# All engine orders, buffer places and engine choices of a fused attention and channel-mix kernel written anew

## The chip, the cores and the metric

The kernel runs on one core of one Trainium2 chip. The metric is the device time of one execution in microseconds (us). Three runs of the kernel before took 166.07, 166.12 and 166.47 us; the median is 166.12 us. Matrix products run on TensorE (PE; PEld is its weight load), elementwise work on VectorE (DVE), ScalarE (ACT) and GpSimd (POOL), and SyncE (SP) issues nearly all transfers. SBUF is the on-chip memory that all of them read; PSUM holds the results of PE.

## The reference

The reference is windowed attention with four sink positions, and behind it a channel mix with a token shift. The inputs q, k and v are 4 batches x 8 heads x 768 positions x 64, in float32.

```python
keep = (pos[None, :] < 4) | ((rel >= 0) & (rel < 128))      # rel = query - key
scores = where(keep, scale * q @ k.T, -1e9)                 # scale = 1/8
x = softmax(scores) @ v                                     # heads side by side: (4, 768, 512)
x_prev = x shifted by one position, zeros at the start
xk = mu_k * x + (1 - mu_k) * x_prev
xr = mu_r * x + (1 - mu_r) * x_prev
kk = maximum(xk @ w_k, 0) ** 2                              # 512 -> 1024
out = sigmoid(xr @ w_r) * (kk @ w_v)                        # 1024 -> 512
```

## The kernel before, in words

The work is cut into 12 units of 256 positions (4 batches x 3), numbered 0 to 11. A unit goes through four stages, and the stages of neighbouring units run at the same time.

- **Prepare.** ks, qs and vs are loaded in float32 (256 KB to each transfer, issued by SP). Casts to bfloat16 make kb, qb (lines 536 and 543, two halves each) and vb (line 646, two halves). kb and qb are then turned into kt and qt, either by PE through a PSUM bank (line 576) with a copy out of it (line 589), or by a transposing transfer on SP's queue (line 562): k of units 4 to 11 and q of units 8 to 11 go the second way.
- **Attend.** In four chunks of two heads: scores on PE into sc (line 721), exponential on ACT into e (line 775), a mask on DVE (line 789), values on PE (line 808), reciprocal and scaling on DVE into x (lines 822 and 825). Units 0 and 1 have no mask on DVE; PE adds a bias to sc ahead of the scores (line 728) from a tile that GpSimd builds at the start (line 418, named ob there). Sink keys are copied by GpSimd into ksink once per batch (line 670).
- **Mix.** x is transposed into xt (line 849, or by transfer in units 9 to 11), td is the difference of neighbouring positions (line 877), and xk and xr are each built by four scalar-tensor-tensor instructions (line 888).
- **Channel mix.** Keys on PE (line 939), rl by a relu out of the bank (line 949 on ACT or 953 on DVE), kk by a square (line 967 on ACT or 963 on DVE), the gate on PE (line 979) with a tanh on ACT (line 985), the value product on PE (line 997, and 909 for the last 128 positions), and one DVE instruction that multiplies both (lines 1006 and 919) ahead of the store. The weights wk, wr and wv come in float32 and are cast once, at the start (lines 501, 505 and 507).

While PE would be idle early on, it multiplies a tile of zeros named warm (line 1018), which I call fills below.

Nothing decides the order at run time. Every step is recorded as an operation with a number, and three tables written out by hand or by a planner decide the rest. `CHOICE` gives the engine for the operations that have a choice, `SLOTS` the buffer of each tile in the order of recording, and `ORDER` the sequence in which operations are emitted; a negative number is a fill. Each engine runs its own instructions in that sequence and waits in place when an input or a buffer is not ready. The four `bank` buffers, the two `sc` buffers and the SP queue are the scarcest. In the names of the order rows below, the digit behind a tile's name is its buffer, not its unit.

Of the kernel before, what the change touches and what calls it, by code (L numbers as in the profile page):

```python
# [18 lines left out]
    92: "ACT", 93: "ACT", 94: "ACT", 95: "ACT", 97: "ACT", 100: "ACT", 102: "DVE", 105: "DVE",  # L19
    110: "DVE", 111: "DVE", 114: "ACT", 115: "DVE", 139: "POOL", 142: "POOL", 145: "POOL", 148:  # L20
    "DVE", 150: "DVE", 151: "ACT", 152: "ACT", 154: "DVE", 161: "DVE", 191: "DVE", 193: "DVE",
    194: "DVE", 197: "DVE", 199: "DVE", 200: "DVE", 203: "DVE", 204: "DVE", 213: "DVE", 230:
    "ACT", 234: "ACT", 273: "DVE", 276: "DVE", 279: "DVE", 282: "DVE", 285: "ACT", 286: "ACT",
    298: "DVE", 306: "DVE", 315: "ACT", 354: "DVE", 364: "ACT", 365: "DVE", 367: "DVE", 383:
    "ACT", 387: "ACT", 436: "DVE", 439: "DVE", 444: "DVE", 445: "DVE", 467: "ACT", 475: "ACT",
    514: "DVE", 516: "DVE", 521: "DVE", 524: "ACT", 525: "ACT", 546: "ACT", 550: "ACT", 554:
    "ACT", 558: "ACT", 595: "DVE", 598: "DVE", 603: "ACT", 604: "ACT", 606: "DVE", 634: "ACT",
    681: "DVE", 682: "DVE", 691: "DVE", 700: "ACT", 704: "ACT", 708: "ACT", 755: "DVE", 759:
    "DVE", 760: "ACT", 772: "DVE", 781: "ACT", 785: "ACT", 789: "ACT", 834: "DVE", 836: "DVE",
    837: "DVE", 853: "ACT", 856: "DVE", 857: "ACT", 860: "DVE", 861: "ACT", 904: "DVE", 906:  # L30
    "DVE", 910: "DVE", 912: "DVE", 913: "DVE", 929: "ACT", 933: "ACT", 940: "DVE", 941: "ACT",
    994: "DVE", 995: "ACT", 999: "ACT", 1003: "ACT", 1007: "ACT", 1022: "DVE", 1026: "DVE",
# [113 lines left out]
)  # L146


# [926 lines left out]
```

## Time and profile before

| what | value |
|---|---|
| median of three runs | 166.12 us |
| span of the profiled execution, first to last instruction | 164.3 us |
| median less span | 1.8 us |
| PE busy | 158.4 us in 1603 matrix products, 30 of them fills |
| DVE busy | 145.4 us |
| ACT busy | 131.2 us |
| POOL busy | 13.5 us, 9.9 of them in the first 24 us |
| mean granted TensorE clock | 0.999 |

The profile gives the span of the profiled execution and no other time of it; the 1.8 us are taken as lying outside the first and the last instruction. A line of groups reads: line, engine, operation, output<-input, sizes, count, then busy time in us and mean ns of one, then the idle time of the engine ahead of them and what ended it. A row of the timeline reads: start, duration, engine, line, operation, count. A row of windows has, for every engine, busy us and the number of instructions in that stretch. PE's matrix products overlap in the pipeline and their ends are modelled, so PE's busy share hides short waits.

### The profile page before, as it was taken

The page shows a single profiled execution, that of the slowest core. Times are in us where ns is not written, and L with a number is a line of the kernel's source. Part 1 is how long each engine was busy: PE and PEld are TensorE (multiplying, and loading weights), DVE is VectorE, ACT ScalarE, POOL GpSimd, SP SyncE. Part 2 cuts the span into 40 slices and gives each one's busy share as a digit, 9 for nine tenths or more (in the row PEclk, how much of TensorE's full clock was granted, in tenths as well). Part 3 has the DMA queues.
Part 4 walks back from the last instruction along what each step waited for, and adds up shares of the span by engine and source line. Part 5 has one row for each costly group of instructions (what it writes and reads, how often), then busy time and mean ns, then how long its engine had stood idle before and what let it go on. Part 6 is the DMA issues. An engine that isn't in the chain of part 4 may idle for free.

```text
span 164.3 us, 4195 instructions
## 1 busy us (share of the span) xinstructions
PE 158.4 (96%) x1603; PEld 102.6 (62%) x1603; DVE 145.4 (89%) x381; ACT 131.2 (80%) x218; POOL 13.5 (8%) x38
## 2 busy tenths in 40 slices
PE   6999889999999999999999999999999999999992
PEld 2455568866467587577566775856575765664851
DVE  5259999999999999989999999999999999789752
ACT  3277999999999999999999999997668759163240
POOL 6409300010000000060000000000000000000000
PEclk9999999999999999999999999999999999999999
DMA  4999999999969896999999887986996955077743
GB/s 120 247 305 311 348 335 355 301 354 210 228 154 270 135 240 148 234 198 167 224 216 157 188 156 163 235 146 150 199 123 136 362 149 200 0 90 297 262 185 128
DMA packets 79042, 34.60 MB, mean 211 GB/s; under 512 B 67112, under 2 KB 73520, under 8 KB 79024
## 3 DMA queue, kind: packets, MB, share of 16 engines
q1 hardware_dynamic: 79008, 34.35, 86.3%
q8 instruction: 12, 0.20, 0.6%
q14 instruction: 6, 0.05, 0.1%
q10 hardware_dynamic: 16, 0.00, 0.0%
HBM read 24.12 MB, written 6.29 MB: 185 GB/s over the span
## 4 chain that ended last, share of the span: by engine, by line
PE 79%; ACT 8%; SPq 4%; DMA 3%; issue 2%; DVE 1%; POOL 1%; DVEq 0%; ACTq 0%; POOLq 0%
PE bank L997 23%; PE bank L939 23%; PE bank L979 12%; PE bank L808 6%; PE sc L721 6%; SPq L337 3%; DMA qs<-in_q_dram 3%; PE bank L576 2%; ACT e L775 2%; PE bank L849 2%; ACT rl L949 1%; PE bank L763 1%; ACT qt L589 1%; PE bank L909 1%; PE bank L1018 1%
## 5 line engine op out<-in xcount | busy, mean ns | idle before, releaser
L775 ACT ACTIVATE e<-sc 128x1024 bf16<-128x1024 f32 (+1 forms) x48 | 46.1, 994 | 1.8 <-PE sc L721 1.7
L939 PE MATMUL bank<-xk,wk_sb 128*128 128x256 bf16 x384 | 47.1, 273 | 0.0
L997 PE MATMUL bank<-wv_h,kk 128*128 128x512 bf16 x184 | 43.1, 379 | 0.1
L939 PEld LDWEIGHTS <-wk_sb 128*128 128x128 bf16 x384 | 36.4, 98 | 7.4 <-issue 0.4
L949 ACT ACTIVATE rl<-bank 128x512 bf16<-128x512 f32 x40 | 24.2, 625 | 8.6 <-PE bank L939 7.1
L997 PEld LDWEIGHTS <-kk 128*128 128x128 bf16 x184 | 17.1, 98 | 17.8 <-issue 0.4
L789 DVE TENSOR_TENSOR e<-e,mask 128x1024 bf16<-128x1024 bf16 (+1 forms) x40 | 25.4, 642 | 0.7 <-ACT e L775 0.5
L979 PE MATMUL bank<-wr_sb,xr 128*128 128x512 bf16 x96 | 23.7, 379 | 0.0
L888 DVE SCALAR_TENSOR_TENSOR xk<-td,mu_all,xt 128x256 bf16<-128x256 bf16 x48 | 22.4, 483 | 0.3
L888 DVE SCALAR_TENSOR_TENSOR xr<-td,mu_all,xt 128x256 bf16<-128x256 bf16 x48 | 22.1, 475 | 0.2
L967 ACT ACTIVATE kk<-rl 128x512 bf16<-128x512 bf16 x29 | 18.3, 664 | 4.2 <-DVE rl L953 4.0
L985 ACT ACTIVATE th<-bank 128x512 f32<-128x512 f32 x24 | 15.1, 646 | 5.7 <-PE bank L979 5.7
L825 DVE TENSOR_TENSOR x<-bank,rec 128x256 bf16<-128x256 f32 x48 | 19.2, 416 | 0.4
L808 PE MATMUL bank<-vb,e 128*128 128x65 bf16 x352 | 16.6, 194 | 0.0
L1006 DVE SCALAR_TENSOR_TENSOR w<-th,bank 128x512 f32<-128x512 f32 x19 | 13.0, 682 | 3.6 <-issue 1.8
L808 PEld LDWEIGHTS <-e 128*128 128x128 bf16 x352 | 13.6, 97 | 3.5
L979 PEld LDWEIGHTS <-xr 128*128 128x128 bf16 x96 | 8.8, 98 | 8.6 <-issue 0.2
L721 PE MATMUL sc<-qt,kt 64*128 64x128 bf16 (+1 forms) x256 | 13.9, 238 | 0.0
L721 PEld LDWEIGHTS <-kt 64*128 64x128 bf16 x256 | 8.9, 94 | 5.7 <-issue 3.1
L1018 PE MATMUL bank<-warm 128*128 128x512 bf16 x30 | 10.6, 484 | 1.1 <-DVE warm L1038 1.1
L877 DVE TENSOR_TENSOR td<-xt 128x512 bf16<-128x512 bf16 x24 | 10.3, 428 | 0.7 <-ACT xt L858 0.5
L589 ACT COPY qt<-bank 128x512 bf16<-128x512 bf16 x15 | 9.4, 643 | 1.0 <-PE bank L576 1.0
(74 smaller groups left out, 161.7 us busy)
## 6 DMA issues: line engine op xcount, KB each, us to landing
ks<-in_k_dram SPq DMA_DIRECT2D x24, 256.0 KB, 4.7
qs<-in_q_dram SPq DMA_DIRECT2D x24, 256.0 KB, 4.4
vs<-in_v_dram SPq DMA_DIRECT2D x24, 256.0 KB, 4.4
out_dram<-w SPq DMA_DIRECT2D x19, 256.0 KB, 2.7
w<-in_moe_w_k_dram SPq DMA_DIRECT2D x2, 1024.0 KB, 10.4
w<-in_moe_w_v_dram SPq DMA_DIRECT2D x2, 1024.0 KB, 9.3
w<-in_moe_w_r_dram SPq DMA_DIRECT2D x1, 1024.0 KB, 9.7
out_dram<-ob SPq DMA_DIRECT2D x4, 256.0 KB, 2.6
```

The source lines that it names most:

```text
L721: nc.tensor.matmul(out=sc[:, a, o0:o1], lhsT=lhs[rows], rhs=rhs[rows], start=u not in BIAS, stop=True, skip_group_check=u in BIAS)
L775: nc.scalar.activation(out=buf[ek][:, :, lo:], in_=buf[sck][:, :, lo:], func=AF.Exp, scale=scale)
L789: nc.vector.tensor_tensor(out=at, in0=at, in1=m, op=ALU.mult)
L808: nc.tensor.matmul(out=o[:, g, a, :], lhsT=e[:, a, e0:e0 + 128], rhs=rhs, start=(T == 0 and i == 0), stop=(i == len(blocks) - 1), skip_gro ...
L825: P.op("DVE", dve(256), lambda ok=ok, rk=rk, c=c: nc.vector.tensor_tensor(out=buf["x", u][:, :, 128 * c:128 * c + 128].rearrange("p g (a d ...
L888: nc.vector.scalar_tensor_tensor(out=buf[key][:, c, :], in0=buf[tk][:, i, :], scalar=mu[w][:, c:c + 1], in1=xt[:, c, t0 - 1:t0 + 255], op0 ...
L939: nc.tensor.matmul(out=ps[:, i, :], lhsT=wk_sb[:, c, 128 * f:128 * f + 128], rhs=xk[:, c, :], start=(c == 0), stop=(c == NC - 1), skip_gro ...
L949: nc.scalar.activation(out=buf[rk], in_=buf[psk].rearrange("p (i t) -> p i t", i=2), func=AF.Relu)
L967: nc.scalar.activation(out=buf["kk", u][:, 2 * f2:2 * f2 + 2, :], in_=buf[rk], func=AF.Square)
L979: nc.tensor.matmul(out=buf[psk], lhsT=buf["xr", u][:, c, 128 * g:128 * g + 128], rhs=wr_sb[:, c, :], start=(c == 0), stop=(c == NC - 1))
L985: P.op("ACT", act(512), lambda psk=psk, tk=tk: nc.scalar.activation(out=buf[tk], in_=buf[psk], func=AF.Tanh, scale=0.5), rank + 4 + g, tak ...
L997: nc.tensor.matmul(out=buf[psk], rhs=wv_h[:, f, :], lhsT=buf["kk", u][:, f, 128 * g:128 * g + 128], start=(f == 0), stop=(f == NF - 1))
```

## The change

The code is the same apart from the three tables, which are longer by 13 lines in all: line N of the kernel before is line N+13 after. What the program does is the same set of operations, with the same loads, products and stores. What differs:

```diff
 CHOICE = {
-    92: "ACT", 93: "ACT", 94: "ACT", 95: "ACT", 97: "ACT", 100: "ACT", 102: "DVE", 105: "DVE",
...
+    92: "DVE", 93: "ACT", 94: "ACT", 95: "POOL", 96: "DVE", 97: "DVE", 98: "ACT", 99: "DVE", 100:
...
 ORDER = (
-    80, 81, 78, 82, 87, 83, 84, 77, -1, -2, -3, -4, -1, -2, 90, 0, 1, 79, 102, 108, -2, -3, -4,
...
+    80, 82, 87, 77, 89, 83, 2, 3, 0, 1, 81, 4, -1, -2, -3, -4, -1, -2, -3, -4, -1, -2, 119, 5, 79,
...
 SLOTS = (
-    0, 0, 0, 1, 1, 0, 1, 1, 2, 0, 1, 2, 2, 2, 0, 0, 0, 1, 1, 1, 2, 2, 0, 0, 0, 2, 1, 1, 1, 2, 2,
...
+    0, 0, 0, 1, 1, 1, 0, 1, 2, 1, 0, 2, 2, 2, 0, 0, 0, 1, 1, 1, 2, 2, 0, 0, 0, 2, 1, 1, 1, 2, 2,
...
```

Counted over the whole program, the instructions that change engine are these:

| instruction | ACT | DVE | POOL |
|---|---|---|---|
| casts to kb | 11 to 5 | 11 to 12 | 2 to 7 |
| casts to qb | 9 to 9 | 14 to 11 | 1 to 4 |
| casts to vb | 11 to 7 | 13 to 10 | 0 to 7 |
| copies to kt and qt | 20 to 22 | 4 to 2 | |
| weight casts (128x1024) | 6 to 4 | 4 to 5 | 0 to 1 |
| relu to rl | 40 to 42 | 8 to 6 | |
| square to kk | 29 to 31 | 19 to 17 | |

The change is described as having casts on GpSimd for the first two units alone. The tables say otherwise: the kernel before has three such casts, all for unit 1, and the changed one has 19, of which seven are for units 0 and 1, one is a weight's, and eleven are for units 3 to 11. The fills go from 30 to 20. SP loads q of the first units ahead of k, the second half of w_k ahead of the first, and it issues the first stores among the loads and no longer behind most of them.

The first place is GpSimd's queue from the bias tile (ob) on. Before, with the casts of unit 1 and three pairs of ksink copies behind them:

```order
L418 AFFINE_SELECT ob2_134<-warm_144 128x128 x2
L451 COPY spread_149<-ident_148 4x4x4 x2
L543 CAST qb1_83<-qs1_71 128x2x4x64
L543 CAST kb1_80<-ks1_68 128x2x4x64
L418 AFFINE_SELECT mask_146<-ones_157 128x128 x2
L543 CAST kb1_80<-ks1_68 128x2x4x64
L470 COPY vsink0_153<-hmask_150 128x8
L470 COPY vsink1_154<-hmask_150 128x8
L670 COPY ksink0_151<-kt0_85 64x4x4 x2
```

After, the same stretch, which begins with the mask that is now built ahead of the bias:

```order
L431 AFFINE_SELECT mask_146<-ones_157 128x128 x2
L431 AFFINE_SELECT ob2_134<-warm_144 128x128 x3
L447 MEMSET ob2_134 4x256
L483 COPY vsink0_153<-hmask_150 128x8
L483 COPY vsink1_154<-hmask_150 128x8
L556 CAST qb0_82<-qs0_70 128x2x4x64
L659 CAST vb0_135<-vs0_73 128x8x64
L464 COPY spread_149<-ident_148 4x4x4 x2
L556 CAST kb0_79<-ks0_67 128x2x4x64
L556 CAST qb1_83<-qs1_71 128x2x4x64
```

The mask's two instructions stand ahead of the bias, and halves of q, v and k of unit 0 come in as casts.

The second place is the rest of GpSimd's queue, which lies in the part of the run where all units are in flight. Before it is only copies of sink keys:

```order
L418 AFFINE_SELECT mask0_147<-ones_157 128x128 x3
L434 MEMSET mask0_147 4x256
L670 COPY ksink1_152<-kt3_88 64x4x4 x2
L670 COPY ksink0_151<-kt2_87 64x4x4 x2
L670 COPY ksink1_152<-kt1_86 64x4x4 x2
```

After, casts of k, q and v stand between those copies:

```order
L549 CAST kb1_80<-ks1_68 128x512
L659 CAST vb2_137<-vs2_75 128x8x64
L549 CAST kb0_79<-ks2_69 128x512
L683 COPY ksink0_151<-kt2_87 64x4x4 x2
L549 CAST qb2_84<-qs2_72 128x512
L549 CAST kb0_79<-ks2_69 128x512
L683 COPY ksink1_152<-kt0_85 64x4x4 x2
L659 CAST vb2_137<-vs1_74 128x8x64
L549 CAST kb2_81<-ks1_68 128x512
```

Casts that DVE and ACT did for the later units now wait their turn on GpSimd.

The third place is ACT's queue at the start, from its first cast. Before:

```order
L543 CAST kb0_79<-ks0_67 128x2x4x64
L589 COPY kt0_85<-bank1_64 128x2x256
L589 COPY qt0_89<-bank2_65 128x2x256
L646 CAST vb0_135<-vs0_73 128x8x64
L775 ACTIVATE e0_93<-sc0_61 128x2x384
L775 ACTIVATE e1_94<-sc1_62 128x2x384
```

After:

```order
L602 COPY qt0_89<-bank0_63 128x2x256
L387 DMA ob2_134<-in_moe_mu_r_dram 4x128
L602 COPY kt0_85<-bank2_65 128x2x256
L602 COPY qt0_89<-bank1_64 128x2x256
L788 ACTIVATE e0_93<-sc0_61 128x2x384
L788 ACTIVATE e1_94<-sc1_62 128x2x384
```

Two casts ahead of the first exponential have left ACT, a copy to qt has come ahead of it, and one small load was moved behind a copy.

More of the change, by code (lines that the diff above doesn't have):

```diff
@@ L25 @@
[L25 to L30, printed above, removed]
@@ L31 @@
[L31 to L32 removed]
+    92: "DVE", 93: "ACT", 94: "ACT", 95: "POOL", 96: "DVE", 97: "DVE", 98: "ACT", 99: "DVE", 100:
+    "ACT", 101: "DVE", 102: "DVE", 104: "ACT", 105: "DVE", 107: "ACT", 108: "POOL", 110: "ACT",
+    111: "POOL", 113: "ACT", 114: "POOL", 115: "DVE", 139: "DVE", 141: "ACT", 142: "DVE", 144:
+    "DVE", 145: "POOL", 147: "ACT", 148: "POOL", 150: "ACT", 151: "POOL", 152: "POOL", 154: "DVE",
@@ new lines @@
+    161: "DVE", 191: "DVE", 193: "ACT", 194: "DVE", 196: "DVE", 197: "DVE", 199: "ACT", 200:
+    "ACT", 202: "ACT", 203: "DVE", 204: "DVE", 206: "DVE", 213: "DVE", 221: "ACT", 222: "ACT",
+    225: "ACT", 226: "DVE", 229: "DVE", 230: "ACT", 233: "ACT", 234: "ACT", 273: "DVE", 275:
+    "ACT", 276: "DVE", 278: "ACT", 279: "DVE", 281: "ACT", 282: "POOL", 284: "ACT", 285: "ACT",
+    286: "ACT", 291: "DVE", 298: "ACT", 306: "ACT", 307: "DVE", 310: "ACT", 311: "DVE", 314:
+    "ACT", 315: "ACT", 318: "ACT", 319: "ACT", 354: "DVE", 356: "DVE", 358: "ACT", 359: "ACT",
@@ new lines @@
+    361: "ACT", 363: "ACT", 364: "ACT", 365: "DVE", 367: "ACT", 374: "ACT", 382: "ACT", 383:
+    "DVE", 386: "ACT", 387: "ACT", 390: "ACT", 391: "ACT", 394: "ACT", 395: "ACT", 434: "ACT",
+    436: "ACT", 438: "ACT", 439: "POOL", 441: "ACT", 443: "ACT", 444: "DVE", 445: "DVE", 447:
+    "DVE", 454: "ACT", 462: "ACT", 463: "ACT", 466: "ACT", 467: "DVE", 470: "ACT", 471: "DVE",
+    474: "ACT", 475: "ACT", 514: "DVE", 516: "ACT", 518: "ACT", 519: "DVE", 521: "DVE", 523:
+    "ACT", 524: "POOL", 525: "DVE", 530: "DVE", 537: "ACT", 545: "ACT", 546: "ACT", 549: "ACT",
@@ L33 @@
+    1007: "DVE", 1022: "DVE", 1023: "ACT", 1026: "DVE", 1027: "DVE", 1030: "ACT", 1031: "DVE",
     1034: "DVE", 1035: "ACT",
```

17 lines of the change are left out of this document (12 added, 5 removed), and 155 rows, old and new, of tables (ORDER, SLOTS).

## The prediction

> **What bounds the kernel now.** I read the page's first part, then the busy time by stage, then the chain of waits, then single instructions where GpSimd and DVE meet.
>
> ```profile
> span 164.3 us, 4195 instructions
> PE 158.4 (96%) x1603; PEld 102.6 (62%) x1603; DVE 145.4 (89%) x381; ACT 131.2 (80%) x218; POOL 13.5 (8%) x38
> ```
>
> PE is the fullest engine, but DVE is close. The stages say where:
>
> ```profile
> 13.00:24.00 11.00, 9.73 (x141) 6.21 (x140) 10.67 (x31) 10.21 (x17) 4.87 (x13) 1.00 1.09 338
> 24.00:60.00 36.00, 35.96 (x384) 24.66 (x385) 35.40 (x93) 35.70 (x59) 0.74 (x2) 1.00 0.98 253
> 60.00:100.00 40.00, 39.89 (x443) 27.27 (x440) 38.16 (x103) 39.57 (x71) 2.89 (x4) 1.00 0.97 190
> 100.00:140.00 40.00, 40.00 (x425) 25.67 (x423) 39.01 (x100) 32.02 (x52) 0.00 (x0) 1.00 0.85 183
> 140.00:161.00 21.00, 21.00 (x145) 13.34 (x142) 15.65 (x35) 7.59 (x13) 0.00 (x0) 1.00 0.52 163
> ```
>
> The columns behind the window's length are PE, PEld, DVE, ACT and POOL. From 24 to 140 us DVE is busy 35.40 + 38.16 + 39.01 = 112.57 of 116 us: it idles 3.4 us in all. ACT is as full until 100 us. So three engines run side by side with hardly a gap, each fed by the others. Only from 140 us on is PE alone, with DVE and ACT in reserve. The chain shows the same:
>
> ```profile
> 65.14 0.93 ACT e L775
> ...
> 68.26 0.49 ACT th L985
> ...
> 148.10 3.45 PE bank L997 x16
> ...
> 152.41 3.49 PE bank L939 x32
> ...
> 159.36 1.76 PE bank L909 x16
> 161.15 0.42 DVE w L919
> ```
>
> Around 65 us it runs over ACT, at the end over PE without a pause, and then the last DVE instruction and its store up to 164.3. PE's products are the same before and after, so the time can move in three places: the start, the waits between 24 and 140 us, and the end. The last is the same in both: the two half products of line 909, two short DVE instructions, two stores. I put it at nothing, since from 140 us PE covers all other work; if that cover went, it would show as idle PE there.
>
> **What DVE and ACT are relieved of.** Prices from the groups:
>
> ```profile
> L646 DVE CAST vb<-vs 128x512 bf16<-128x512 f32 x13 | 5.4, 420 | 0.1
> ...
> L953 DVE TENSOR_SCALAR rl<-bank 128x512 bf16<-128x512 f32 x8 | 5.5, 685 | 1.5 <-PE bank L939 1.5
> ...
> L536 ACT CAST kb<-ks 128x512 bf16<-128x512 f32 x10 | 6.6, 655 | 0.0
> ...
> L501 ACT ACTIVATE wk_sb<-w 128x1024 bf16<-128x1024 f32 x4 | 4.2, 1092 | 0.0
> ```
>
> From the table of the change, DVE loses net 7 instructions of the short kind (2 qb and kb, 3 vb, 2 squares) at 0.42 us and 3 of the long kind (2 copies to kt and qt, 2 relus, less one weight cast) at 0.685: 2.9 + 2.1 = 5.0 us. ACT loses net 4 of the 512-column kind (10 casts, less 2 copies, 2 relus, 2 squares) at 0.655 and 2 weight casts at 1.092: 2.6 + 2.2 = 4.8 us. The means include the tail of an instruction in which the next one already runs, so both sums are upper values. By themselves they would let PE run with fewer waits.
>
> **What GpSimd's casts cost.** GpSimd's casts go from 3 to 19. Four of them (q, v and k of unit 0, q of unit 1) fall before about 13 us, where DVE waits for loads anyway. Of the other 15 the kernel before has two. That is 13 more, and the weight's cast is twice as wide, so 14 at the price of one. The price has two sides: how long GpSimd takes, and how long it holds up DVE.
>
> ```profile
> L543 POOL CAST kb<-ks 128x512 bf16<-128x512 f32 x2 | 1.4, 702 | 0.0
> L543 POOL CAST qb<-qs 128x512 bf16<-128x512 f32 x1 | 0.9, 865 | 6.7 <-DMA qs<-in_q_dram 6.7
> ...
> 13.48 0.62 POOL L543 CAST kb<-ks 128x512 bf16<-128x512 f32 x1
> ...
> 15.01 0.79 POOL L543 CAST kb<-ks 128x512 bf16<-128x512 f32 x1
> ...
> 13.75 0.62 DVE L877 TENSOR_TENSOR td<-xt 128x512 bf16<-128x512 bf16 x1
> ...
> 15.34 0.73 DVE L888 SCALAR_TENSOR_TENSOR xk<-td,mu_all,xt 128x256 bf16<-128x256 bf16 x1
> ...
> L877 DVE TENSOR_TENSOR td<-xt 128x512 bf16<-128x512 bf16 x24 | 10.3, 428 | 0.7 <-ACT xt L858 0.5
> ...
> L888 DVE SCALAR_TENSOR_TENSOR xk<-td,mu_all,xt 128x256 bf16<-128x256 bf16 x48 | 22.4, 483 | 0.3
> ```
>
> The td that met the first cast took 0.62 us where the mean is 0.43; the xk that met the second took 0.73 where the mean is 0.48. Both end the same 0.27 us behind the cast (14.37 after 14.10, 16.07 after 15.80), so DVE seems to have stood still until GpSimd was done. These two lost 0.19 and 0.25 us because they began when the cast was well under way. The other direction is in the middle of the run, where GpSimd only copies 64x16 sink keys:
>
> ```profile
> L670 POOL COPY ksink<-kt x8: 188/196/2303, 16.2 to 96.6; 64x16 bf16<-64x16 bf16 x8
> ...
> 70.30 2.54 POOL L670 COPY ksink<-kt 64x16 bf16<-64x16 bf16 x2 [36.96 <-DMA kt<-kb]
> ...
> 70.25 0.42 DVE L646 CAST vb<-vs 128x512 bf16<-128x512 f32 x1
> 70.59 0.42 DVE L543 CAST qb<-qs 128x512 bf16<-128x512 f32 x1
> 70.93 0.41 DVE L963 TENSOR_TENSOR kk<-rl 128x512 bf16<-128x512 bf16 x1
> 71.26 1.28 DVE L789 TENSOR_TENSOR e<-e,mask 128x1024 bf16<-128x1024 bf16 x2
> 73.05 0.18 DVE L822 RECIPROCAL rec<-bank 128x4 f32<-128x4 f32 x1 [0.51 <-ACT qt L589]
> ```
>
> Columns of the first row are the shortest, the median and the longest in ns. One copy took 2.30 us instead of 0.19: it was issued at 70.30 and ended at 72.60, as DVE's row of back-to-back instructions out of SBUF ended (72.54). So a GpSimd cast in the full part of the run can wait some 2 us, and when it does get its turn, DVE waits.
>
> The page "SBUF — State Buffer" of the Trainium skill, section "Who interferes with whom", states that DVE and GpSimd share one pair of ports as an exclusive lock, that whoever comes first keeps it for its whole instruction, and that DVE takes it for casts and for two inputs out of SBUF but not for one input out of PSUM. By that rule, the trace agrees: the held instructions above are of the first kinds.
>
> Bounds for the loss of DVE per cast: 0.22 us (mean of the two rows above) and 0.62 us (the whole of the shortest cast). Could it be below nothing? No: a cast on GpSimd frees DVE's time, but that is counted above already. In the middle of the run DVE issues back to back, so a cast gets its turn only at a boundary between two instructions and then stands in the way from its first moment; the value is nearer the upper end, yet DVE's instructions out of PSUM (x, reciprocals, relus) can pass. I take 0.45: 14 x 0.45 = 6.3 us, with ends of 3.1 and 8.7. Less the 5.0 relieved, DVE gains 1.3 us of work, with ends of -1.9 and +3.7. With 3.4 us of idle time in 116, all of it waits for others, I let the whole of it reach the end: PE waits for xk, masks and x.
>
> What sits behind: a late vb holds a value product on PE; a late kb holds the transposing transfers on SP's queue and each load and store queued behind them. Loads are issued well ahead, so I add nothing there, up to 2 us for each cast that is late by as much as the copy above.
>
> **The start.**
>
> ```profile
> 7.04 0.39 PE L576 MATMUL bank<-ident,kb 128*128 128x128 bf16 x4
> ...
> 9.54 0.50 PE L721 MATMUL sc<-qt,kt 64*128 64x256 bf16 x8
> ...
> 4.86 0.44 DVE L543 CAST kb<-ks 128x512 bf16<-128x512 f32 x1 [1.43 <-DMA ks<-in_k_dram]
> ...
> 7.61 0.43 DVE L543 CAST qb<-qs 128x512 bf16<-128x512 f32 x1 [2.31 <-DMA qs<-in_q_dram]
> ...
> 4.68 0.30 POOL L434 MEMSET ob<- 4x256 bf16 x1
> ...
> L418 POOL TENSOR_SCALAR_AFFINE_SELECT mask<-ones 128x128 bf16<-128x128 bf16 x5 | 2.0, 429 | 0.1
> ```
>
> The first scores at 9.54 need both k and q; the second of them arrives at 7.6, whichever it is, so loading q first changes nothing there. The bias tile, whole at 4.98 before (the memset's end), comes 2 x 0.43 = 0.9 us later, behind the mask, and is now PE's first real work; at 5.9 us it would still be ahead of 7.6. The transposes of q's other half now wait for a GpSimd cast (0.6 to 0.9 us by the rows above) where DVE had one of 0.42. Against that, ACT and DVE have less ahead of them up to 24 us, and ten fills fewer are queued; a fill fills a wait and costs nothing in itself. I put the start at 0, with ends of -0.8 (ACT rid of two casts) and +0.9 (the mask's delay passed on).
>
> **The sum.** 164.3 + 1.3 + 0 = 165.6 us of span. The profiled execution's span lies 1.8 us under the median, so 167.4 us.
>
> **The rivals.**
>
> A, faster: GpSimd's casts slip between DVE's instructions out of PSUM and cost 0.22 each. Then DVE is relieved by 1.9 us and ACT by up to 4.8, and PE's waits shrink. Since PE is full of its own work from 100 us on, I let three quarters of the 1.9 through: 164.7 us. For it speaks that the chain runs over ACT around 65 us; against it, the 2.3 us of one tiny copy. It decides if the loss per cast is under 5.0 / 14 = 0.36 us.
>
> B, no change: DVE's relief and loss cancel (0.36 each), and the orders are as good as each other: 166.1 us.
>
> C, much slower: DVE loses the whole cast each time, 8.7 less 5.0 is 3.7: 169.8 us. The lock of the page "SBUF — State Buffer", taken to the letter, gives this if every cast meets a DVE instruction of the locked kinds. Or a late cast stops SP's queue or PE for 2 us once or twice, with the same end.
>
> **The numbers.** The forecast (167.4) has a chance of 0.44, C 0.16, B 0.12, A 0.28. Slower by over 0.3% (0.5 us, about what a measurement can tell here) is then 0.60, within it 0.12, faster 0.28. The range of 164.8 to 170.0 leaves out half of A (0.14) and a third of C (0.05). The slower cases alone lie between 166.7 and 170.0.
>
> **What would show it.** GpSimd busy some 12 to 20 us longer, with casts in the middle well over 0.7 us; td, xk, masks and casts on DVE with larger means than 428, 483 and 420 ns; DVE busy no lower than 144 us though ten instructions have left it; ACT near 126. The start is right if the first scores come between 9 and 10.4 us, and the end if PE's last product ends about 3.4 us ahead of the span's end. I am wrong if GpSimd's casts stay at 0.6 us and DVE's means stay put: then A. I am also wrong if the new order leaves PE waiting at places that have nothing to do with GpSimd, which no row of this trace can show.

## The result, and the profile after

The changed kernel takes 177.4 us in the median of four runs (176.7 to 178.2) beside 166.2 for the kernel before on the same chip: 1.067 of it, with a 95% interval of 1.062 to 1.071. The forecast was 167.4, in a range of 164.8 to 170.0. The sign was right and the size was not: 1.2 us were forecast, 11.2 came. The execution profiled is one of the slower ones, 178.2 us, with a span of 176.5.

The first part of the page after, and the share of the DMA engines over the span in 40 slices:

```profile
span 176.5 us, 4175 instructions
...
PE 158.6 (90%) x1575; PEld 102.3 (58%) x1593; DVE 144.8 (82%) x371; ACT 128.2 (73%) x212; POOL 23.8 (13%) x54
...
DMA  3999999799997996698899997799454560067243
```

No engine has more work than before: PE 158.6 us (158.4 before), DVE 144.8 (145.4), ACT 128.2 (131.2). GpSimd has 10 us more, all of it beside the others. (PE's figure holds 7.8 us of fills instead of 10.6; its other products are the same ones and take 3.0 us longer by the profile, some of them at a lower clock, see the last section.) So nearly all of the 12.2 us of span is waiting. Where, the busy time by stage tells; first the kernel before, then the one after (columns: window, PE, PEld, DVE, ACT, POOL, granted clock, share of the DMA engines, GB/s; the share adds up the times of all packets over 16 engines, so it can pass 1):

```profile
0.00:24.00 24.00, 21.48 (x217) 11.69 (x218) 16.75 (x54) 16.31 (x26) 9.86 (x32) 1.00 0.94 277
24.00:50.00 26.00, 25.96 (x272) 18.02 (x272) 25.52 (x66) 25.80 (x43) 0.74 (x2) 1.00 0.97 268
50.00:90.00 40.00, 39.89 (x438) 26.97 (x435) 38.30 (x102) 39.69 (x70) 2.50 (x2) 1.00 0.99 197
90.00:130.00 40.00, 40.00 (x427) 26.45 (x427) 39.08 (x103) 34.21 (x58) 0.39 (x2) 1.00 0.92 179
130.00:160.00 30.00, 30.00 (x252) 18.75 (x249) 24.75 (x59) 15.18 (x25) 0.00 (x0) 1.00 0.56 181
```

```profile
0.00:24.00 24.00, 19.92 (x208) 10.97 (x210) 16.32 (x51) 14.32 (x23) 11.45 (x37) 1.00 0.89 268
24.00:50.00 26.00, 25.07 (x244) 16.59 (x244) 24.95 (x61) 24.86 (x42) 3.63 (x4) 1.00 1.03 277
50.00:90.00 40.00, 35.49 (x392) 23.76 (x396) 33.38 (x88) 33.23 (x58) 3.85 (x7) 0.96 0.85 201
90.00:130.00 40.00, 35.08 (x371) 23.43 (x375) 34.97 (x89) 32.93 (x55) 4.83 (x7) 1.00 0.95 168
130.00:160.00 30.00, 29.72 (x286) 19.44 (x288) 26.71 (x71) 19.27 (x32) 0.00 (x0) 1.00 0.41 119
```

PE loses 4.4 us from 50 to 90 us (39.89 less 35.49), 4.9 from 90 to 130, 0.9 from 24 to 50 and 0.3 from 130 to 160: 10.5 us. The 1.6 us that it is less busy in the first 24 us are no loss: its fills there are 7.15 us instead of 10.48, its other products 12.8 instead of 11.0, and a kernel below that is as fast as the one before (a_quart) is busy 20.1 us there too. DVE and ACT idle in the same stretches, so none of the three holds up the others by its work. The last column but one was there before the change too: the DMA engines' share is 0.92 to 0.99 up to 130 us. After the change it is 0.85 from 50 to 90 us, where PE waits 4.5 us, so a high share alone doesn't make an engine wait.

The chain that ended last, by engine, before and after:

```profile
PE 79%; ACT 8%; SPq 4%; DMA 3%; issue 2%; DVE 1%; POOL 1%; DVEq 0%; ACTq 0%; POOLq 0%
...
PE 57%; DMA 14%; SPq 11%; DVE 10%; ACT 4%; issue 3%; ACTq 0%; DVEq 0%
```

A quarter of it is now transfers and SP's queue (DMA and SPq), where it was 7%. Some of the waits of the engines for transfers (us in total, times, longest), before and then after:

```profile
POOL qb L543 <- DMA qs<-in_q_dram: 6.7, 1, 6.7
...
DVE qb L543 <- DMA qs<-in_q_dram: 2.3, 1, 2.3
...
ACT kb L543 <- DMA ks<-in_k_dram: 1.7, 1, 1.7
...
DVE kb L543 <- DMA ks<-in_k_dram: 1.4, 1, 1.4
```

```profile
PE sc L734 <- DMA qt<-qb: 3.3, 2, 2.1
...
ACT qb L556 <- DMA qs<-in_q_dram: 3.2, 1, 3.2
...
DVE kb L556 <- DMA ks<-in_k_dram: 3.0, 2, 2.8
...
DVE vb L659 <- DMA vs<-in_v_dram: 2.5, 2, 1.3
...
PE bank L589 <- ACT qb L556: 2.3, 1, 2.3
...
ACT qb L549 <- DMA qs<-in_q_dram: 1.7, 1, 1.7
```

Before, DVE and ACT wait 5.4 us for loads, all at the start. After, the row of DVE's kb and one of the two waits of vb are at the start as well, but from 15 us on DVE and ACT wait 8.0 us for loads of q, k and v where they waited for none before, and PE itself stands at a score product for a transposed q. One of them, followed back along SP's queue (the timeline of SP, start, duration, instruction; after):

```profile
49.66 0.57 SPq L320 DMA_DIRECT2D vs<-in_v_dram  x1
50.29 1.33 SPq L350 DMA_DIRECT2D qs<-in_q_dram  x2
51.66 0.61 SPq L330 DMA_DIRECT2D ks<-in_k_dram  x1
52.32 2.65 SPq L320 DMA_DIRECT2D vs<-in_v_dram  x1
55.02 1.49 SPq L330 DMA_DIRECT2D ks<-in_k_dram  x1
56.55 0.92 SPq L320 DMA_DIRECT2D vs<-in_v_dram  x1
57.51 0.79 SPq L350 DMA_DIRECT2D qs<-in_q_dram  x1
```

and the chain of waits goes on from there:

```profile
57.51 3.78 DMA qs<-in_q_dram
...
61.37 0.13 ACT qb L556
```

By the order of the program, the row at 50.29 holds the first half of q of unit 5 and the first half of q of unit 6; the row at 57.51 is the second half of q of unit 5. Between them stand q, k and v of unit 6, k of unit 7 and v of unit 5. ACT waits 3.2 us for that half, until 61.3, and PE waits 2.3 us for ACT's cast before unit 5's transposes (both rows above). Before, both halves of that q were issued one behind the other at 49.0. Half of the loads from 24 us on take 0.66 us or less to issue (0.60 before); here three of them took 2.65, 1.49 and 0.92.

For all 48 half loads of units 4 to 11, the time from their issue on SP's queue to the first cast that reads them, worked out from both traces:

| | least | median | most | under 4.9 us |
|---|---|---|---|---|
| before | 5.0 | 8.1 | 15.4 | 0 |
| after | 3.4 | 7.7 | 31.4 | 7 |

The mean lead is no shorter (8.7 before, 9.4 after). It is uneven: v of unit 9 is issued 31 us ahead of its cast and k of unit 11 29 us, while seven others have at least 0.5 us less than the least that any had before. Three of the seven are read by GpSimd, four by DVE or ACT.

### The profile page after: what moved, and what is told of

The parts are those of the page before. It is cut to its first block, busy times and chain, and to the rows that moved or that the text cites. A ratio compares the mean times of both kernels' runs of the same rounds, so it can differ in the third digit from the quotient of the medians.

```text
span 176.5 us, 4175 instructions
## 1 busy us (share of the span) xinstructions
PE 158.6 (90%) x1575; PEld 102.3 (58%) x1593; DVE 144.8 (82%) x371; ACT 128.2 (73%) x212; POOL 23.8 (13%) x54
## 4 chain that ended last, share of the span: by engine, by line
PE 57%; DMA 14%; SPq 11%; DVE 10%; ACT 4%; issue 3%; ACTq 0%; DVEq 0%
PE bank L952 19%; PE bank L1010 15%; PE bank L992 8%; DMA qs<-in_q_dram 5%; SPq L350 4%; PE sc L734 4%; PE bank L821 4%; SPq L320 4%; DMA qt<-qb 3%; DMA vs<-in_v_dram 3%; DMA ks<-in_k_dram 3%; DVE x L838 2%; PE bank L862 2%; SPq L330 2%; DVE td L890 1%
## 5 line engine op out<-in xcount | busy, mean ns | idle before, releaser
L952 PE MATMUL bank<-xk,wk_sb 128*128 128x256 bf16 x384 | 49.1, 278 | 2.0 <-ACT th L998 2.0
L788 ACT ACTIVATE e<-sc 128x1024 bf16<-128x1024 f32 (+1 forms) x48 | 44.3, 955 | 2.4 <-PE sc L734 2.4
L952 PEld LDWEIGHTS <-wk_sb 128*128 128x128 bf16 x384 | 37.0, 99 | 9.6 <-issue 2.2
L802 DVE TENSOR_TENSOR e<-e,mask 128x1024 bf16<-128x1024 bf16 (+1 forms) x40 | 26.4, 669 | 3.1 <-ACT e L788 3.1
L901 DVE SCALAR_TENSOR_TENSOR xr<-td,mu_all,xt 128x256 bf16<-128x256 bf16 x48 | 23.1, 485 | 0.0
L998 ACT ACTIVATE th<-bank 128x512 f32<-128x512 f32 x24 | 14.4, 606 | 9.1 <-PE bank L992 8.7
L980 ACT ACTIVATE kk<-rl 128x512 bf16<-128x512 bf16 x31 | 19.3, 637 | 1.9 <-DVE rl L966 1.8
L1019 DVE SCALAR_TENSOR_TENSOR w<-th,bank 128x512 f32<-128x512 f32 x19 | 12.8, 681 | 4.0 <-PE bank L1010 2.9
L835 DVE RECIPROCAL rec<-bank 128x4 f32<-128x4 f32 x48 | 7.5, 172 | 7.4 <-PE bank L821 6.7
L890 DVE TENSOR_TENSOR td<-xt 128x512 bf16<-128x512 bf16 x24 | 11.2, 478 | 1.8 <-DMA xt<-x 1.7
L602 ACT COPY qt<-bank 128x512 bf16<-128x512 bf16 x14 | 8.4, 599 | 4.2 <-PE bank L589 4.1
(76 smaller groups left out, 158.6 us busy)
```

Of the source, the lines that this page charges most:

```text
L788: nc.scalar.activation(out=buf[ek][:, :, lo:], in_=buf[sck][:, :, lo:], func=AF.Exp, scale=scale)
L802: nc.vector.tensor_tensor(out=at, in0=at, in1=m, op=ALU.mult)
L901: nc.vector.scalar_tensor_tensor(out=buf[key][:, c, :], in0=buf[tk][:, i, :], scalar=mu[w][:, c:c + 1], in1=xt[:, c, t0 - 1:t0 + 255], op0 ...
L952: nc.tensor.matmul(out=ps[:, i, :], lhsT=wk_sb[:, c, 128 * f:128 * f + 128], rhs=xk[:, c, :], start=(c == 0), stop=(c == NC - 1), skip_gro ...
L980: nc.scalar.activation(out=buf["kk", u][:, 2 * f2:2 * f2 + 2, :], in_=buf[rk], func=AF.Square)
L998: P.op("ACT", act(512), lambda psk=psk, tk=tk: nc.scalar.activation(out=buf[tk], in_=buf[psk], func=AF.Tanh, scale=0.5), rank + 4 + g, tak ...
```

## The experiments

The theories: G, GpSimd's casts cost what was lost; E, the orders of PE, DVE and ACT themselves are worse; L, loads and transposing transfers land late; within L, whether their order on SP's queue alone is at fault or what the engines' orders ask of it. The expectations also name Q (a bad order on SP's queue alone), S (the early stores), P (the places in SP's queue and not the bytes) and M (what one transfer gains another loses, or each order of transfers fits one order of casts). Times are medians beside the kernel before on the same chip (166.0 to 166.5). All kernels differ from the changed kernel or the one before only as shown; where SP's queue is altered, the other engines' orders and choices are untouched. In the diffs, q5.1 is the second half load of q of unit 5, kt and qt are transposing transfers, S a store.

### GpSimd's casts

Taken off GpSimd in the changed kernel, and put on GpSimd in the kernel before:

```diff
 # changed kernel -> a_nogps; kernel before -> b_gps is the reverse
-    282, 439, 524, 593, 679, 751, 755, 836, 837, 904, 912: "POOL"
+    282, 439, 755, 836, 837, 904, 912: "DVE",  524, 593, 679, 751: "ACT"
```

> The changed kernel with the eleven casts of units 3 to 11 that stand on GpSimd given to the engine that had them in the kernel before (seven to VectorE, four to ScalarE), at the same places of the order; nothing else is moved. Theory G: the loss of the change comes from these casts, so the time falls by 6 us or more, to 168 to 171.5. Theory Q: the casts are 0.6 to 0.8 us long in the trace, GpSimd is idle before them waiting for the loads, so the same late loads now hold VectorE and ScalarE, which have other work queued behind: 177 to 180, slower than the changed kernel.

> The kernel before with the eleven casts of units 3 to 11 that the changed kernel has on GpSimd given to GpSimd at their places, seven taken from VectorE and four from ScalarE; nothing else is altered. Theory G: the lock or the length of the casts costs 0.45 us each and what waits for them, 168.5 to 172. Without such a cost VectorE has 2.9 us and ScalarE 2.2 us less to do where both are full: 163.5 to 166.1. In between (165.8 to 167) the relief and the cost of the lock are about even, as the prediction had it.

Measured (ratios are to the kernel before, with a 95% interval): a_nogps 180.1 us (178.8 to 181.8), ratio 1.082 [1.076, 1.088], slower than the changed kernel; b_gps 166.35, ratio 1.002 [0.9996, 1.004]. Theory G falls from both sides. b_gps also gives the price of a cast on GpSimd, which the prediction had estimated. Its page, and two groups of DVE:

```profile
span 164.8 us, 4208 instructions
...
PE 158.4 (96%) x1603; PEld 102.3 (62%) x1603; DVE 146.4 (89%) x374; ACT 130.0 (79%) x214; POOL 21.5 (13%) x49
```

```profile
L804 DVE TENSOR_TENSOR e<-e,mask 128x1024 bf16<-128x1024 bf16 (+1 forms) x40 | 26.1, 663 | 0.9 <-ACT e L790 0.8
L903 DVE SCALAR_TENSOR_TENSOR xk<-td,mu_all,xt 128x256 bf16<-128x256 bf16 x48 | 23.2, 501 | 0.3
```

DVE has seven casts fewer, 7 x 0.42 = 2.9 us, and yet is busy 146.4 us instead of 145.4: its other work grew by 3.9 us, the masks from 642 to 663 ns in the mean, xk from 483 to 501. That is 3.9 / 11 = 0.36 us for each cast on GpSimd, and PE's time does not move. The other way round, a_nogps gives DVE these seven casts back and its busy time goes from 144.8 to 145.0 us, so its other work shrinks by 2.7 us, 0.25 for each cast, in a kernel where DVE idles more. And b_gps too has seven leads under 4.9 us, six of them of loads that GpSimd reads, at the time of the kernel before: a short lead costs nothing where the reader can wait.

### The bytes of the loads

Each load of units 3 to 11 cut to a quarter of its rows, in both kernels, and to a half in the changed one (shown: v; q and k alike):

```diff
-                        out=buf[key][:, g, :, :],
-                        in_=v[b, :, s0:s0 + 128, :].rearrange("h p d -> p h d")), rank,
+                        out=buf[key][:, g, 0:H if u < 3 else 2, :],
+                        in_=v[b, 0:H if u < 3 else 2, s0:s0 + 128, :].rearrange(
+                            "h p d -> p h d")), rank,
```

> The changed kernel with each load of q, k and v of units 3 to 11 cut to a quarter of its rows (the other three quarters of the buffer keep what an earlier unit left there, so attention of these units is computed on partly stale data); number and order of the transfers, casts and products are as they were. Theory L (the loads arrive late because SP's queue issues them in an order that leaves the DMA engines, busy 0.8 to 1.1 of the time up to 120 us, too little time for what is wanted next): with a quarter of the bytes nearly every transfer is early, and the time falls to within 3 us of the same cut made in the kernel before, 164 to 169. Theory E (the orders of VectorE, ScalarE and TensorE themselves are worse): at least 6 us above the cut kernel before, 171 to 176. Theory P (the places of the transfers in the in-order queue, with their waits, not the bytes): 171 to 177, with TensorE waiting at the same places.

> The kernel before with the same cut of each load of units 3 to 11 to a quarter of its rows (attention on partly stale data). The profile of before shows no wait of VectorE, ScalarE or TensorE for a load after the start, so all theories say 163 to 166.5; a gain of more than 3 us would mean that the full queue of transfers costs the kernel before something too.

> The changed kernel with each load of units 3 to 11 cut to half of its rows (attention of these units on partly stale data). If the DMA engines are only a little short of what the order asks (they are busy 0.8 to 1.1 of the time to 120 us), half of the bytes is enough and the time is that of the quarter, 166 to 167.5; if they are far short, half of the loss stays, 169 to 173.

Measured: a_quart 166.3 us, ratio 1.001 [0.998, 1.004]; b_quart 166.0, 0.998 [0.996, 1.001]; a_half 167.5, 1.007 [1.004, 1.009]. With a quarter of the bytes the changed kernel takes the time of the kernel before, and the cut gives the kernel before nothing. The engines' orders, their choices, GpSimd's casts and the number and places of the transfers are the same in a_quart as in the changed kernel; so E and G fall as causes by themselves, and the whole loss comes with transfers that land late. The window from 50 to 90 us in a_quart:

```profile
50.00:90.00 40.00, 39.65 (x468) 27.69 (x467) 39.61 (x103) 38.40 (x66) 6.36 (x9) 1.00 0.47 100
```

The DMA engines are busy 0.47 of the time there and PE waits 0.35 us, against 4.51. Half of the bytes leaves 1.2 us of the 11, so the shortage is not a large one. A quarter of the bytes is also a quarter of the packets, and SP issues faster: from 24 us on 52 loads of q, k and v take 53.5 us to issue in the changed kernel (47.7 in the one before), 51 take 28.1 in a_quart. So this cut doesn't part the DMA engines from the queue that feeds them.

The same cut in units 3 to 7 alone (a_q37), and in units 8 to 11 alone (a_q811):

```diff
-                        out=buf[key][:, g, 0:H if u < 3 else 2, :],
+                        out=buf[key][:, g, 0:H if u < 3 or u > 7 else 2, :],   # a_q37
+                        out=buf[key][:, g, 0:H if u < 8 else 2, :],            # a_q811
```

> The changed kernel with the loads of units 3 to 7 alone cut to a quarter of their rows (attention of these units on partly stale data). Read from the trace of the changed kernel, TensorE waits 8.8 us from 50 to 90 us (1.8 in the kernel before) and 7.2 us from 90 to 130 us (1.3 in the kernel before). If each wait belongs to the loads of its own stretch, the cut takes away the first 7 us: 170 to 172. If the first half's backlog is also what makes the second half late, 166.5 to 169.

> The changed kernel with the loads of units 8 to 11 alone cut to a quarter of their rows. If each wait belongs to the loads of its own stretch, it takes away the second 6 us and a little of the first (some loads of units 8, 9 and 11 are issued between 66 and 92 us): 169 to 171.5. If the waits of the first half come back later as waits that were hidden behind the second, 172 to 175.

Measured: a_q37 169.55 us, ratio 1.018 [1.013, 1.022]; a_q811 168.3, 1.010 [1.006, 1.014]. Gains of 7.9 and 9.1, more together than the 11.1 of both at once, so the two halves share a part. In each, the stretch whose loads were left whole keeps waits; a_q37 first:

```profile
50.00:90.00 40.00, 39.33 (x461) 27.52 (x465) 39.31 (x103) 38.45 (x66) 5.20 (x9) 1.00 0.78 150
90.00:130.00 40.00, 37.35 (x399) 23.89 (x404) 36.79 (x97) 31.75 (x54) 3.56 (x4) 1.00 0.84 167
```

```profile
50.00:90.00 40.00, 37.37 (x438) 25.69 (x442) 37.18 (x98) 36.30 (x63) 4.92 (x9) 1.00 0.82 177
90.00:130.00 40.00, 39.40 (x430) 25.89 (x434) 39.34 (x105) 34.57 (x57) 2.83 (x4) 1.00 0.43 104
```

PE still waits 2.7 us behind 90 us in the first and 2.6 us ahead of it in the second, over half of what the changed kernel waits there (4.9 and 4.5): the rest of each wait went with loads of the other half, which stood in the way.

### Stores among the loads

```diff
  SP, changed kernel -> a_stores:
- q7.1 S0.0 kt6.1 k7.1 S1.1 q8.0 ... q10.1 S4.0 kt10.1 ... v11.0 S3.0 ... kt11.0 S6.0 kt11.1
+ q7.1 kt6.1 k7.1 q8.0 ... q10.1 kt10.1 ... v11.0 ... kt11.0 kt11.1 S0.0 S1.1 S4.0 S3.0 S6.0
  SP, kernel before -> b_stores: S0.0, S1.1, S4.0, S3.0 put behind q7.1, k7.1, q11.1, kt11.0
```

> The changed kernel with the five stores that stand among the loads on SP's queue (issued at 68.6, 72.8, 113.2, 117.4 and 128.4 us) moved behind the last transposing transfer of k; nothing else is moved. Theory S: each store takes 0.6 us of issue and waits up to 2.3 us for its product; two of them stand ahead of late transfers of unit 6, 7, and two ahead of those of unit 10, so 2 to 4 us come back: 173.5 to 175.5. Theory Q: a part of its own sum, 0.5 to 2 us back: 175.4 to 177. Theory G: no change, 176.7 to 178.

> The kernel before with four stores (ob of units 0, 1, 4 and 3) put among the loads at the places that the changed kernel has for them on SP's queue; nothing else is moved. Each store moves 256 KB, some 1.3 us at the 190 GB/s of the stretch from 60 to 120 us. Theory L with leads: the loads of before are issued at least 5.0 us ahead of their cast, 8.2 in the median, so two stores in a row are mostly swallowed: 166 to 168. If the place of a store in the queue, with its wait for its product, holds what is behind it: 168 to 172.

Measured: a_stores 174.45 us, ratio 1.051 [1.044, 1.058], 3 us of the 11 back; b_stores 166.0, ratio 0.999 [0.997, 1.002]. Five such stores cost 3 us in the changed kernel's queue; four cost nothing in the queue of before, whose loads of units 4 to 11 have at least 5.0 us of lead.

### Single transfers put forward

```diff
  SP, changed kernel -> a_five (a_five_st: and the stores as in a_stores):
- q5.0 q6.0 k6.0 v6.0 k7.0 v5.0 q5.1        ... q6.1 k9.0 ... v9.0 v6.1
+ q5.0 q5.1 q6.0 k6.0 v6.0 k7.0 v5.0        ... q6.1 v6.1 k9.0 ... v9.0
- qt8.0 v8.0 v8.1 k10.1 kt8.1 qt8.1         ... q10.0 ... q11.1 q10.1
+ qt8.0 qt8.1 v8.0 v8.1 k10.1 kt8.1         ... q10.0 q10.1 ... q11.1
- qt10.0 v11.0 S3.0 qt10.1
+ qt10.0 qt10.1 v11.0 S3.0
  SP, changed kernel -> a_halves: each second half directly behind its first, 27 moved
```

> The changed kernel (177.4 us) with one thing altered: on SP's queue the load of the second half of each unit's q, k or v (27 of them) stands directly behind the load of its first half; the orders of TensorE, VectorE, ScalarE and GpSimd, the engine choices and the buffers are as they were. Theory Q (SP's queue is in a bad order: a half that is needed soon is issued behind loads that are needed later and behind transposing transfers and stores): the TensorE waits at 58.1 (2.5), 62.3 (1.6), 83.5 (1.4) and 115.9 (1.5 us) hang on second halves of q of unit 5, v of unit 7 and q of unit 10, 7.0 us together, so 170 to 173 us, and the stretch from 60 to 120 loses most of its TensorE waits. Theory G (the casts on GpSimd are what costs, by the lock or by their length): no change, 176.7 to 178. Theory S (the early stores on SP's queue): no change either, 176.5 to 178.

> The changed kernel with five transfers moved forward on SP's queue and nothing else: the second half of q of unit 5 behind its first (issued at 57.5 us in the trace, six transfers behind it), the second half of v of unit 6 behind that of q of unit 6 (79.0 us, 27 us behind its first half), the second transposing transfer of q of unit 8 behind the first (99.3 us, 16 us after its cast), the second half of q of unit 10 behind its first (112.2 us), and the second transposing transfer of q of unit 10 behind the first (118.9 us). Theory L in the form that single transfers stand too late behind ones that are wanted later: the TensorE waits at 58.1, 62.3, 83.5, 99.9, 115.9 and 120.5 us (10.5 us) go in good part, 168 to 173. If the DMA engines are so full that what is put forward makes another transfer late by as much (theory M): 175 to 181.

> The same five transfers put forward, and the five early stores moved behind the last transposing transfer of k. Theory L: what the stores gave (3 us) beside the five, 167 to 170.5. Theory M: 172 to 178.

Measured: a_halves 180.4 us (178.1 to 181.0), ratio 1.082 [1.073, 1.091]; a_five 173.1, 1.039 [1.033, 1.045]; a_five_st 173.8, 1.047 [1.042, 1.052]. The five transfers bring 4.3 us, the stores nothing beside them. Putting all second halves forward, for which theory Q expected 170 to 173, makes it worse; theory L's reading is that what is put ahead of its need takes the time of what is needed. The page "DMA: Bandwidth & Descriptors" of the Trainium skill, section "Rules for kernel authors", says to issue a transfer early and wait for it late; a_halves, with 27 loads issued ahead of others, takes 3.0 us more than the changed kernel, so here that was not free.

### The two orders of SP's queue exchanged

```diff
  a_sp_before: changed kernel, SP's rows in the order (and q, k, v buffers) of the kernel before
  b_sp_after:  kernel before, SP's rows in the order (and buffers) of the changed kernel
```

> The changed kernel with SP's queue in the order that it had in the kernel before (loads of q, k and v on the buffers of before; eleven transfers, mostly stores, a place or a few later than there, where the order of the engines asks it). TensorE, VectorE, ScalarE and GpSimd keep the orders and choices of the changed kernel. Theory Q (SP's order alone): 167 to 171. Theory E (the orders of the engines themselves: casts, products and chains placed so that they wait): 175 to 179. Theory M (neither order is bad in itself; the two were made for one another, and a load that comes early for one is late for the other): 178 to 190.

> The kernel before with SP's queue in the order of the changed kernel (buffers of q, k and v as there; four transfers a place or two later, where the order of the engines asks it); TensorE, VectorE, ScalarE and GpSimd keep the orders and choices of before. Theory Q: 171 to 177. Theory E: 166 to 168. Theory M: 174 to 190.

Measured: 205.8 us and 211.0, ratios 1.238 [1.232, 1.244] and 1.271 [1.265, 1.277]. Both lie above every expectation (at most 190). Neither order is good or bad by itself. Each fits one order of casts, and with the other's it costs 28 us (over the changed kernel) and 45 (over the kernel before). The likely way, read from the orders and not run by itself: an engine that meets a cast whose load is further back in the queue stops with all that stands behind the cast, and SP stops at a transfer whose cast or buffer isn't ready.

### Whole orders by need

```diff
  SP, changed kernel, all transfers sorted by the time at which their reader wants them:
  a_need  from the trace after, as early as buffers allow (q, k, v buffers of the kernel before)
  a_edf   from the trace after less its waits, as late as the DMA engines allow
  a_due   from a_quart's trace, 3.6 us + own time ahead (transposing: 4.6), at most 16 ahead
  a_both  a_due up to q8.1, then a_five_st with v9.0, k11.0, kt8.1, kt9.0 moved to their need
```

> The changed kernel with the whole of SP's queue put into another order: loads in the order of the units on the buffers that the kernel before gave them, each half behind the other, transposing transfers as soon as their casts are made, loads and transfers sorted by when their first reader stands in the order, stores last unless a buffer is wanted. TensorE's, VectorE's, ScalarE's and GpSimd's orders and the engine choices are those of the changed kernel. Theory Q: all TensorE waits that hang on DMA in the trace come back (58.1, 62.3, 66.1, 83.5, 99.9, 115.9, 120.5: 11.2 us), less what the next wait takes, so 167 to 170. Theory G: 176 to 178. If the orders of the engines themselves are at fault (theory E: first kp product at 26.1 against 24.0 us, and other engine waits), 171 to 175.

> The changed kernel with SP's queue put in order once more: each transfer stands by the time at which its first reader wants it in the trace of the changed kernel (the waits taken out), less its own duration, and as late as the DMA engines can do it (1.25 us a load, 1.4 a transposing transfer, 3.0 a weight block); the two weight blocks of w_v stand early again, the stores behind 120 us. Everything else is as in the changed kernel. Theory L or P: the waits for loads go, 168 to 172. Theory E: 173 to 178. If the order of casts in the changed kernel leaves no good order of loads (theory M), 175 to 185.

> The changed kernel with the transfers after the weight blocks of w_v in order of need as the trace of the kernel with quartered loads shows it (there nothing is late, so the readers' times are those that the engines' own orders ask): each load 3.6 us and its own 0.8 to 1.3 us ahead of its reader, each transposing transfer 4.6 us ahead, both halves of k's and q's transposes together, none sooner than 16 us ahead, stores behind 121 us. Engines' orders, choices and buffers as in the changed kernel. Theory L1 (the transfers' order alone is bad and a good one exists for these engine orders): 165.5 to 169.5. Theory L2 (these engine orders want the loads in another order than the buffers come free, or more of them in one stretch than the DMA engines carry, so no order of transfers mends it): 171 to 178.

> The changed kernel with SP's queue put together from the two orders that mended one half each: up to the second half of q of unit 8 the order by need (TensorE busy 39.3 of 40 us from 50 to 90 us there), behind it the order with five transfers put forward and late stores (39.2 of 40 us from 90 to 130 us there), with v of unit 9, k of unit 11 and the transposing transfers of k of units 8 and 9 put where their readers want them. Engines' orders, choices and buffers as in the changed kernel. Theory L1 (a good order of transfers exists for these engine orders): 166.5 to 169.5. Theory L2 (these engine orders want the loads sooner than the DMA engines, busy 0.85 to 1.1 of the time to 120 us, can carry them: by 100 us 63 of 72 half loads, by 105 us 65, where the kernel before wants 59; a half that is mended moves the shortage into the other): 171 to 176.

Measured: a_need 187.3 us, 1.132 [1.123, 1.140]; a_edf 185.6, 1.113 [1.106, 1.120]; a_due 175.4, 1.052 [1.045, 1.058]; a_both 173.7, 1.048 [1.041, 1.055]. The first two are bad orders of mine, a_need outside every expectation, and show how much one place is worth. In a_need the weights of w_v stood behind loads of units 4 and 5 and were issued at 43.6 us; from 40 to 50 us no engine ran:

```profile
40.00:50.00 10.00, 0.00 (x0) 0.00 (x0) 0.00 (x0) 0.00 (x0) 0.00 (x0) 0.67 0.95 248
```

In a_edf one half of a transposed k came 5.7 us late:

```profile
PE sc L736 <- DMA kt<-kb: 7.8, 2, 5.7
```

The other two tell more. a_due mends the first stretch and a_five_st the second; a_both was to have both (rows of a_due, of a_five_st and of a_both):

```profile
50.00:90.00 40.00, 39.33 (x464) 27.31 (x463) 38.84 (x102) 38.28 (x65) 4.14 (x7) 1.00 1.05 185
90.00:130.00 40.00, 34.50 (x363) 21.68 (x361) 35.64 (x93) 30.79 (x52) 3.94 (x6) 1.00 0.89 148
```

```profile
50.00:90.00 40.00, 36.67 (x402) 24.66 (x406) 34.71 (x92) 34.73 (x60) 4.79 (x9) 0.96 1.12 201
90.00:130.00 40.00, 39.24 (x443) 26.05 (x447) 39.13 (x100) 34.30 (x57) 3.08 (x4) 1.00 0.94 181
```

```profile
50.00:90.00 40.00, 39.25 (x462) 27.63 (x466) 39.23 (x102) 38.66 (x66) 4.73 (x8) 1.00 1.16 197
90.00:130.00 40.00, 35.11 (x381) 22.54 (x385) 35.07 (x90) 30.31 (x51) 3.82 (x6) 1.00 1.07 185
```

Where the first stretch runs without waits, the second is short of 5 us, with a DMA share of 1.05 to 1.16 ahead of it. That is what theory L2 expected (171 to 178 and 171 to 176). The share alone doesn't say which stretch will be short: a_five_st has 1.12 in the first one and no lack in the second. The reason that L2 gives can be counted in a_quart's trace, where nothing is late: the engines' orders of the changed kernel read 51 of the 72 half loads by 80 us, 60 by 95, 65 by 105 and 71 by 115; those of before 46, 55, 59 and 64. They ask for five to seven half loads more by the same time. Of the five by 80 us three are read by casts on GpSimd, which can wait, and two by casts in the rows of DVE and ACT; of the seven by 115 us four and three. At 256 KB a piece and 190 GB/s five are 6.9 us of transfers, by estimate.

What stays open: four whole orders were tried by need and the best of them, a_both, brought 3.7 us; five transfers put forward brought 4.3. That no order does better isn't shown. That early casts of DVE and ACT make the shortage was counted, not run: no kernel with those casts alone put back was made. And a_quart takes bytes off every load at once, so it doesn't tell waiting for the bytes from waiting in the queue behind the bytes of others, nor full DMA engines from an SP queue that issues for 34.3 of the 40 us from 50 to 90 us (36.0 in the kernel before).

## Why the prediction was wrong

**The step that failed** is "Loads are issued well ahead, so I add nothing there". It was set at nothing and measured 11.1 us (177.4 less 166.3 of a_quart). The rows of before that I quoted for the windows carried the DMA engines' share, 0.98 from 24 to 60 us, 0.97 to 100 and 0.85 to 140, and I named the columns up to POOL and read no further. With that share, a change which re-orders the loads is a change to a resource that is nearly full; that no engine waited for a load before (5.4 us, all at the start) showed only that the order of before fitted. What the runs showed in place of the step: loads issued as late as 3.6 us ahead of a cast on DVE, and 8.0 us of waits of DVE and ACT for loads from 15 us on.

- **What bounds the kernel.** Right for PE, DVE and ACT; the fourth that was nearly full, the transfers (DMA engines and SP's queue), was missed.
- **The relief.** 5.0 us for DVE and 4.8 for ACT, called upper values. In a_quart ACT is busy 128.0 us, 3.2 less than before, and DVE 144.7, 0.7 less, the relief and the casts' price together.
- **GpSimd's casts.** 0.45 us each was taken between 0.22 and 0.62; b_gps measures 0.36 (0.25 from a_nogps), just the price at which rival B put relief and loss even. It came out even there: 166.35. In the changed kernel six of the ten casts on GpSimd from 50 us on took 0.6 to 0.7 us, and one at 31 us took 2.0; DVE's td went from 428 to 478 ns. GpSimd was busy 10.3 us longer, where 12 to 20 were named. That DVE pays for each cast was right, the size 0.09 too high, 1.3 us over 14 casts.
- **What sits behind.** The late casts were to hold SP's queue by up to 2 us each. In the trace after, SP's queue waits for GpSimd once, for 0.3 us. It went the other way: GpSimd idles 78 us in all ahead of its casts for loads of q, k and v, so the casts came late because their loads did.
- **The start.** First scores at 9.62 us (9.54 before), within 9 to 10.4. The first product with w_k begins at 25.9 us (24.0 before), and at 25.8 in a_quart too, where the time is that of before; so that delay cost nothing in the time.
- **The end.** PE's last products run from 171.44 to 173.35 and the span ends at 176.5, 3.2 us later: right.
- **The sum and the rivals.** Without the late loads the changed kernel takes 166.3 us: rival B to 0.2 us, and 1.1 below the forecast. C (169.8, a cast that stops SP's queue once or twice) came nearest in the number and had the wrong cause. What was named as the way to be wrong, PE waiting at places that have nothing to do with GpSimd, is what happened; "no row of this trace can show" was not quite true, since the share of the DMA engines gave a sign of it. That the kernel got slower, as forecast, was luck: the forecast's cause, GpSimd's casts, cost nothing on balance (b_gps).

## What to carry to other kernels

Read the DMA engines' share in each stage beside those of the other engines: where it is near 1, as here (0.92 to 0.99), a transfer is a place in line, and one moved ahead of its need can put a later one behind its own. The share doesn't say by itself who will wait. Before a change of orders is priced, take the lead of each load (issue to first reader) before, see which engine reads it and whether that one can wait, and compare the new order of casts with the new order of loads; what an order that wants a few loads sooner costs is not seen in the busy time of the engine that was re-ordered. To find out whether transfers are at fault, cut their bytes and leave all else: two runs settled what eleven re-orderings of SP's queue did not.

## What was not expected of the hardware

- SP's issue itself can be slow: a load's issue took 3.95 us at 24.41, behind weight blocks and with a DMA share of 1.07 from 24 to 28 us, where the median from 24 us on is 0.66, and while it lasts nothing behind it on the queue moves. The same load took 3.72 us in a_quart, where it has a quarter of its bytes (at 20.58; share 1.06 from 20 to 24 us), and the loads from 28.7 to 32.5 us were issued in 0.5 to 0.8 us each there (share 0.94 from 28 to 33 us). So a slow issue goes with what is already under way more than with the size of the load; why is not shown.

```profile
24.41 3.95 SPq L350 DMA_DIRECT2D ks<-in_k_dram  x1
```

- A wait of PE can cost more than its length. PE waits 2.3 us up to 62.04 and 0.65 us up to 63.97; from 64 to 67 us the granted clock is 0.50, and there the products with w_k follow each other every 213 ns instead of 109 (eight take 1.86 us from 63.97, eight took 1.04 from 62.28). From 60 to 70 us the clock is 0.83 in the mean, and in the gap of a_need 0.67 (row above); the kernel before has 1.00 from 24 to 160 us.

```profile
63.97 1.86 PE bank L952 x8
...
60.00:70.00 10.00, 7.30 (x77) 5.70 (x78) 5.29 (x14) 7.31 (x12) 0.60 (x2) 0.83 0.82 197
```

- From 50 to 90 us the DMA share is 0.99 before the change for 197 GB/s, where 1.11 moved 342 from 20 to 30 us (the row of before). Most packets are small (the page after). Counted in the trace of before, 24265 of the 26478 packets from 50 to 90 us have 256 bytes and take 21 ns in the mean, those of 1024 bytes 53 ns.

```profile
20.00:30.00 10.00, 9.50 (x132) 7.47 (x129) 9.83 (x28) 10.00 (x15) 0.00 (x0) 1.00 1.11 342
```

```profile
DMA packets 79043, 34.61 MB, mean 196 GB/s; under 512 B 67112, under 2 KB 73520, under 8 KB 79024
```

The page "DMA: Bandwidth & Descriptors" of the Trainium skill, section "Specifications", gives 512 B as the least for full rate; by that, the trace agrees.
